# Stage a and stage b of a spectral filter, in pairs of pieces between the projections of an attention

## The chip, the cores and the metric

One core of one Trainium2 chip runs the whole kernel. The metric is the device time of one execution in microseconds; the time before is the median of three runs, 651.31 us.

## The reference

Two independent halves, both with 2048 rows and 448 columns, written side by side:

```python
# a: attention, 16 heads of 28, one shared key and value head
q = (x @ wq) -> 16 heads of 28;  k = x @ wk;  v = x @ wv
p = softmax(q k^T * 28 ** -0.5);  a = concat_heads(p v) @ wo
# b: global filter
X = rfft2(B_x)              # over rows and columns
b = irfft2(X * (w_r + 1j * w_i))
out = concatenate([a, b], axis=-1)
```

All inputs and outputs are float32.

## The kernel before

**Attention.** The queries of four heads at a time (group g, 0 to 3) are projected for 512 rows at a time (chunk c, 0 to 3). `proj` issues the matmuls (line 331): each factor is split into a rounded part and a rest, so a group with a chunk takes 11 matmuls of 128 x 512 into one PSUM bank. `evac` (lines 335 and 336) copies the bank to `qraw` on ScalarE and takes the largest magnitude of each row on VectorE into `qmx`. Keys and values ride along in spare rows of the query weights; `fetch` gathers them by DMA into `kf`, and `keys` splits the keys into `ka` (one half of the rows at a time, lines 250 to 256).

Chunk 0 is projected in the order of arrival of its inputs. For chunks 1 to 3 a loop goes over c and g, so that the count `n = 4 * (c - 1) + g` runs from 0 to 11; "group n" means this count. `split_x` prepares the next chunk's input on ScalarE (line 319) and VectorE (lines 321 and 323).

A bound on the scores is subtracted from each query. For it `qm` (line 430) is reduced from `qmx` behind group 9, `key_max` (lines 351 and 352) moves it with two small matmuls and a copy to `kmb`, `terms` (line 260) and `shift` (lines 265 and 266) form `cvec`, and `build_q` (lines 201 to 203) makes the first chunk's query: `qt`, its rounded part `qh`, its rest `ql`. `copy_q` (lines 191 to 194) puts these into the four row blocks of `qa`, on ScalarE, on VectorE and by DMA from the SP and GpSimd queues.

Behind that the main part runs over 256 steps: scores (line 780), exp on ScalarE (line 781), product with the values (line 756), with the rest of the filter and of the output placed between them by a plan written out by hand. It starts at 70.24 us.

**Filter, first part.** It is done in eight pieces q, which lie between the projections:

- `fft1_load(q)` asks for the piece `xb` (512 KB) and for its twiddle weights `fw` (128 KB) on the SP queue, lines 101 and 103.
- `fft1_fold(q)` adds and subtracts mirrored parts on VectorE in eight instructions, lines 113 to 122; it can be done in two parts, four instructions each. Its result `f` lies in one of two buffers.
- Stage a: `fft1_a_mm(q, p)` for p = 0 and 1 is a run of small matmuls (113 x 32 weights, line 138) into one PSUM bank for each p; `fft1_a_out` evacuates each with ScalarE (line 144) to `a`, which has two buffers for each p.
- Stage b: `fft1_mm(q)` multiplies `a` by `fw` (64 x 64 weights, line 157) into two banks; `fft1_out` evacuates them (line 165 on ScalarE for q below 6, line 167 on VectorE above) to `bs`, and stores `bs` to the scratch tensor `t1` from the SP queue (line 172).

Banks for projections, stage a and small matmuls come from `bank()`, which hands out six banks in turn; stage b of pieces 0 to 5 has two banks of its own (`pbb`, `po`).

**Where the pieces stand.** The order on TensorE (PE) is the order of the program text (`manual_schedule`). The other engines and the DMA queues are ordered by a planner, by readiness and text order; `behind(x, y)` tells it to issue x after y on the same engine. Behind the groups in `slots` stand stage a of one piece and stage b of the piece before:

```python
slots = (3, 5, 6, 8, 9, 10)
...
if n in slots:
    q = slots.index(n)
    fft1_a(q)
    fft1_load(q + 4)
    ...
    if q:
        fft1_b(q - 1)
    if n == 9:
        key_max()
```

Piece 6 (stage a), piece 5 (stage b), `shift` of the other chunks, piece 6 (stage b), the reduction of the bound, piece 7 (stage a) and the transposes of the values follow behind group 11 in this order on PE; stage b of piece 7 stands within the first step of the main part.

Of the kernel before, what the change touches and what calls it, by code (L numbers as in the profile page):

```python
# [55 lines left out]
def kernel(ctx: ExitStack, tc: tile.TileContext, t: dict):  # L56
# [21 lines left out]
    def behind(ins, other):  # L78

        tc.add_manual_dep(ins.ins, other.ins.name,  # L80
                          mybir.DependencyInfo(mybir.DependencyClass.NoSync, mybir.DependencyReason.DATA),
                          reason="order of issue")
# [6 lines left out]

    fc, xb, ff = {}, {}, {}
    def fft1_consts():
        fc["cs1"] = fp.tile([128, 4, 113], F32, name="cs1", tag="cs", bufs=1)
        nc.sync.dma_start(fc["cs1"], t["cs1"])

    def fft1_load(q):
        if q > 7:
            return
        x = fp.tile([128, 4, 256], F32, name="xb", tag=("wr", "b2")[q % 2])  # L100
        nc.sync.dma_start(x, t["xb"][q])
        w = fp.tile([128, 4, 64], F32, name="fw", tag=("ph", "pl")[q % 2])
        nc.sync.dma_start(w, t["fw"][:, 4 * q:4 * q + 4])
        xb[q] = x, w

    def fft1_fold(q, part=None):
        x = xb[q][0][:113]
        e2, o2 = x[:, 0:2], x[:, 2:4]
        if part != 1:
            f = ff[q] = fp.tile([113, 4, 4, 2, 32], F32, name="f", tag="wi")  # L110
            xv = x.rearrange("p k (j h m) -> p k j h m", h=2, m=32)
            for h, op in enumerate((ALU.add, ALU.subtract)):
                nc.vector.tensor_tensor(f[:, :, :, h], xv[:, :, :, 0], xv[:, :, :, 1], op=op)
            y = f.rearrange("p k j h m -> p k (j h m)")
            nc.vector.tensor_tensor(e2, y[:, 0::2], y[:, 1::2], op=ALU.add)
            nc.vector.tensor_tensor(o2, y[:, 0::2], y[:, 1::2], op=ALU.subtract)
        if part != 0:
            y = ff[q].rearrange("p k j h m -> p k (j h m)")
            return [nc.vector.tensor_tensor(y[:, 0], e2[:, 0], e2[:, 1], op=ALU.add),
                    nc.vector.tensor_tensor(y[:, 1], e2[:, 0], e2[:, 1], op=ALU.subtract),  # L120
                    nc.vector.tensor_tensor(y[:, 2], o2[:, 0], o2[:, 1], op=ALU.subtract),
                    nc.vector.tensor_tensor(y[:, 3], o2[:, 0], o2[:, 1], op=ALU.add)]

    at1, stored = {}, []

    def fft1_a(q):
        for p in range(2):
            fft1_a_out(q, p, fft1_a_mm(q, p))
# [13 lines left out]
    def fft1_a_out(q, p, pa):  # L142
        a = at1[q, p] = fp.tile([128, 2, DF], F32, name="a", tag=("pwr", "pwi")[p])
        return nc.scalar.activation(a, pa, AF.Copy)

    def fft1_b(q):
        return fft1_out(q, fft1_mm(q))

    def fft1_mm(q, pb=None):
        w = xb[q][1]  # L150
        if pb is None:
            pb = aux2("pbb"), ps_o.tile([128, 2, DF], F32, name="po")
        for p in range(2):
            a = at1.pop((q, p))
            for h in range(2):
                for e in range(2):
                    mm(pb[h][64 * e:64 * e + 64, p], w[64 * h:64 * h + 64, 2 * p + e], a[64 * h:64 * h + 64, e],  # L157
                       start=True, stop=True)
        return pb
# [36 lines left out]
    def build_q(c, g, first=False):  # L196
        cs = slice(c * CW, (c + 1) * CW)
        qh = qp.tile([128, CW], F32R, name="qh", bufs=1)
        ql = qp.tile([128, CW], F32R, name="ql", bufs=1)
        qt = ql.bitcast(F32)  # L200
        nc.vector.tensor_scalar(qt, qraw[:, g, cs], mask, cvec[:, g, c:c + 1], op0=ALU.mult, op1=ALU.add)
        nc.vector.tensor_copy(qh, qt)
        nc.vector.tensor_tensor(ql, qt, qh.bitcast(F32), op=ALU.subtract)
        if (c, g) not in qa:
            qa[c, g] = qp.tile([128, 4, CW], F32R, name="qa")
        q = qa[c, g]
        if first:
            return q, qh, ql
        for i in range(4):
            for p, src in enumerate((qh, ql)):  # L210
                mv = nc.sync.dma_start(q[32 * p:32 * p + 32, i].bitcast(F32), src[32 * i:32 * i + 32].bitcast(F32))
                behind(mv, stored[-1])
        nc.sync.dma_start(q[64:128].bitcast(F32), q[0:64].bitcast(F32))
# [15 lines left out]


    with tc.tile_pool(name="w1", bufs=1) as w1:
        kf = w1.tile([64, S], F32, name="kf")
        qm = w1.tile([128, 2], F32, name="qm")
        prod = w1.tile([128, NG, NC], F32, name="prod")
# [24 lines left out]
        def terms(c0, c1):  # L259
            return nc.vector.tensor_scalar(prod[:, :, c0:c1], qmx[:, :, c0:c1], kmb, None, op0=ALU.mult)  # L260

        def shift(c0, c1):
            b = bank()[:, :NG * (c1 - c0)]
            pb = b.rearrange("p (g c) -> p g c", g=NG)
            mm(b, blk, prod[:, :, c0:c1], start=True, stop=True)
            nc.vector.tensor_copy(cvec[:, :, c0:c1], pb)

        halves = slice(0, 1024), slice(1024, 2048)
        with tc.tile_pool(name="x1", bufs=2) as x1:
# [14 lines left out]
            def raw(src, eng):  # L284
                r = x1.tile([128, 512], F32, name="raw", bufs=8)
                eng.dma_start(r, src)
                return r
# [59 lines left out]
            def key_max():  # L347

                pb = bank()
                for k in range(2):  # L350
                    mm(pb[:, 0:1], sel[:, k], qm[:, k:k + 1], start=(k == 0), stop=(k == 1))
                nc.vector.tensor_copy(kmb, pb[:, 0:1])
# [22 lines left out]
                        proj(pq1[g], *xs[1], g, 0)  # L375
            fft1_consts()
            fft1_load(0)
            xr[2, 0] = raw(t["xa"][2, :, 0], nc.sync)
            for j in range(1, NK):
                split_x(*xs[1], 1, j)  # L380
                xr[2, j] = raw(t["xa"][2, :, j], nc.sync)
            for q in range(1, 4):
                fft1_load(q)
            fft1_fold(0)
            mask = const("mask", [128, 1], nc.sync)
            sgn = const("sgn", [128, 1], nc.sync)
# [7 lines left out]
            for c in range(1, NC):  # L394
                for g in range(NG):
                    pq = pq1[g] if c == 1 else bank()
                    for j in range(1 if c == 1 else 0, NK):
                        proj(pq, *xs[c], g, j)
                    last = evac(c, g, pq)
                    if g == 0 and c < 3:  # L400
                        parts_of(c + 1)
                        for j in range(NK):
                            split_x(*xs[c + 1], c + 1, j)
                            if c < 2:
                                xr[c + 2, j] = raw(t["xa"][c + 2, :, j], nc.sync)
                    if c == 1 and g == 1:
                        fetch(range(7), halves[0])
                    if c == 3 and g == 1:
                        fetch(range(7), halves[1])
                    if c == 2 and g == 3:  # L410
                        fetch(range(7, 14), slice(0, 1536), nc.gpsimd)
                    if c == 3 and g == 2:
                        fetch(range(7, 12), slice(1536, S), nc.gpsimd)
                    if c == 1 and g == 0:
                        fft1_fold(1)
                    if c == 2 and g == 3:
                        keys(0)
                    n = 4 * (c - 1) + g
                    if n in slots:
                        q = slots.index(n)  # L420
                        fft1_a(q)
                        fft1_load(q + 4)
                        if n == 10:

                            terms(0, 1)
                            shift(0, 1)
                            qf, qh, ql = build_q(0, 0, True)
                        if n == 9:

                            top = nc.vector.tensor_reduce(qm, qmx[:, 0:2], axis=AX.X, op=ALU.max)  # L430
                            for ins in fft1_fold(5, 1):
                                behind(ins, top)
                        if q < 6:
                            fft1_fold(q + 2, None if q not in (3, 5) else 0)
                        if q:
                            fft1_b(q - 1)
                        if n == 9:
                            key_max()
            fetch(range(12, 14), slice(1536, S), nc.gpsimd)


        behind(copy_q(0, 1, qf, ql, nc.scalar), last)
        for p in range(2):
            last = fft1_a_out(6, p, fft1_a_mm(6, p))
        for i in range(4):
            copy_q(i, 2, qf, qh, nc.sync)
            copy_q(i, 3, qf, ql, nc.gpsimd)
# [1 line left out]
        top = terms(1, NC)  # L449
        for ins in fft1_fold(7, 1):  # L450
            behind(ins, top)
        last = fft1_b(5)
        shift(1, NC)
        top = nc.vector.tensor_reduce(cmax, cvec, axis=AX.X, op=ALU.max)
        pb6 = fft1_mm(6, [pair_of(bank()) for _ in range(2)])
# [13 lines left out]
            nc.tensor.transpose(pv[:, b], kf[32:64, b * 128:(b + 1) * 128], ident[32:64, 32:64])  # L469
        fft1_out(6, pb6, bound)  # L470
        fft1_a_out(7, 1, pa7)
        nc.vector.tensor_copy(vs, pv)
        keys(1, nc.vector.tensor_copy)


    pools = ctx.enter_context(ExitStack())
# [46 lines left out]
    b2 = {}  # L523
# [494 lines left out]
```

## Time and profile before

| | us |
|---|---|
| three runs | 650.55, 651.31, 651.71 |
| profiled execution | 651.6 |
| its span, first to last instruction | 649.8 |
| TensorE busy | 642.6 (99%) |
| ScalarE busy | 555.9 (86%) |
| VectorE busy | 360.5 (55%) |
| GpSimd busy | 79.6 (12%) |
| mean granted TensorE clock | 0.998 |

Busy times are sums over the whole span; a stretch can have another limit than the mean. The changed code works between 26 and 74 us, before and at the start of the main part. PEld is TensorE's loading of weights, which overlaps its matmuls. A timeline row gives start, duration, engine, line and tiles, a count where like instructions were merged, and in brackets how long the engine had been idle and what ended that.

### The profile page before, as it was taken

The numbers are of one execution on the slowest core, as the hardware profiler recorded it, in microseconds if no ns is written. First come the engines' busy times: TensorE is split into PE (matmuls) and PEld (weight loads), VectorE is DVE, ScalarE is ACT, GpSimd is POOL, SyncE is SP. The second block draws the span as 40 slices with busy tenths as digits, with TensorE's granted clock in tenths as the row PEclk, the third lists the DMA queues.
The fourth block names the chain that finished last, engine by engine and source line by source line (L and its number), as shares of the span: only waits on it lengthen the run. The fifth ranks groups of instructions, "written<-read, shape, count | busy, mean of one in ns | idle before, by whom it ended". The sixth has DMA issues, their size and how long they took to land.

```text
span 649.8 us, 12076 instructions
## 1 busy us (share of the span) xinstructions
PE 642.6 (99%) x4470; PEld 375.8 (58%) x4470; DVE 360.5 (55%) x810; ACT 555.9 (86%) x1103; POOL 79.6 (12%) x150
## 2 busy tenths in 40 slices
PE   8999999999999999999999999999999999999996
PEld 6877554555555456554546556565656565555555
DVE  5999646778877771047765620175443510383523
ACT  5654999999999998789989988799999987899981
POOL 3022401101112100000012200011120200010010
PEclk9999999999999999999999999999999999999999
DMA  8756954534552443022062323032232313140001
GB/s 268 265 172 165 259 159 106 137 100 121 138 139 76 109 95 84 29 75 49 32 155 50 98 60 89 20 88 73 63 94 61 101 39 84 43 110 16 15 31 60
DMA packets 36114, 63.83 MB, mean 98 GB/s; under 512 B 7905, under 2 KB 23922, under 8 KB 35084
## 3 DMA queue, kind: packets, MB, share of 16 engines
q1 hardware_dynamic: 30832, 49.60, 27.6%
q0 software_dynamic: 4640, 12.48, 7.4%
q8 instruction: 36, 0.59, 0.4%
q10 hardware_dynamic: 576, 0.92, 0.4%
q14 instruction: 30, 0.25, 0.1%
HBM read 30.04 MB, written 14.75 MB: 69 GB/s over the span
## 4 chain that ended last, share of the span: by engine, by line
PE 98%; DMA 1%; ACT 0%; SPq 0%; ACTq 0%; issue 0%
PE s L780 30%; PE s L756 24%; PE po L756 7%; PE s L331 6%; PE sx L780 5%; PE po L780 4%; PE sx L756 4%; PE s L677 4%; PE s L138 2%; PE s L623 2%; PE s L611 1%; PE pbb L157 1%; DMA raw<-wq 1%; PE s L521 1%; PE s L519 1%; PE s L520 1%
## 5 line engine op out<-in xcount | busy, mean ns | idle before, releaser
L781 ACT ACTIVATE p<-s 128x512 f32<-128x512 f32 x776 | 421.9, 652 | 38.8 <-PE s L780 38.5
L780 PE MATMUL s<-qa,ka 128*128 128x512 f32 x776 | 243.8, 408 | 0.0
L780 PEld LDWEIGHTS s<-qa,ka 128*128 128x128 f32 x776 | 140.3, 188 | 80.5 <-ACT p L781 43.6
L756 PE MATMUL s<-p,vs 128*32 128x512 f32 x1408 | 163.8, 596 | 0.0
L756 PEld LDWEIGHTS s<-p,vs 128*32 128x32 f32 x1408 | 39.7, 109 | 89.5 <-issue 86.6
L781 ACT ACTIVATE p<-sx 128x512 f32<-128x512 f32 x132 | 86.1, 652 | 3.4 <-PE sx L780 3.4
L781 ACT ACTIVATE p<-po 128x512 f32<-128x512 f32 x116 | 74.9, 646 | 7.2 <-PE po L780 7.1
L658 DVE RECIPROCAL r<-r 128x128 f32<-128x128 f32 x64 | 61.0, 953 | 2.2
L684 DVE COPY ya<-s 128x448 f32<-128x448 f32 x11 | 6.9, 625 | 88.1 <-PE s L677 88.1
L780 PE MATMUL sx<-qa,ka 128*128 128x512 f32 x132 | 53.4, 405 | 0.0
L780 PE MATMUL po<-qa,ka 128*128 128x512 f32 x116 | 47.4, 408 | 0.0
L756 PE MATMUL po<-p,vs 128*32 128x512 f32 x384 | 44.9, 597 | 0.0
L631 POOL TENSOR_TENSOR yo<-y 128x226 f32<-128x226 f32 x16 | 9.6, 597 | 225.9 <-issue 214.8
L780 PEld LDWEIGHTS sx<-qa,ka 128*128 128x128 f32 x132 | 24.8, 188 | 14.0 <-ACT p L781 9.2
L647 POOL DMA_DIRECT2D ol<-ol x36 | 18.1, 508 | 105.4 <-PE s L780 55.9
L756 PE MATMUL sx<-p,vs 128*32 128x512 f32 x256 | 29.7, 596 | 0.0
L780 PEld LDWEIGHTS po<-qa,ka 128*128 128x128 f32 x116 | 21.8, 188 | 12.4 <-ACT p L781 7.0
L625 DVE COPY m<-s 128x452 f32<-128x452 f32 x15 | 9.4, 629 | 34.5 <-PE s L623 34.5
L756 PEld LDWEIGHTS po<-p,vs 128*32 128x32 f32 x384 | 10.7, 109 | 24.1 <-issue 23.4
L331 PE MATMUL s<-xh,wqh 128*128 128x512 f32 x56 | 22.7, 405 | 0.9 <-ACT wqh L311 0.9
L335 ACT ACTIVATE qraw<-s 128x512 f32<-128x512 f32 x14 | 8.1, 600 | 17.4 <-PE s L331 17.4
L331 PE MATMUL s<-xh,wql 128*128 128x512 f32 x56 | 21.6, 391 | 0.0
(211 smaller groups left out, 735.3 us busy)
## 6 DMA issues: line engine op xcount, KB each, us to landing
qa<-qa SPq DMA_DIRECT2D x15, 512.0 KB
raw<-xa SPq DMA_DIRECT2D x16, 256.0 KB
xb<-xb SPq DMA_DIRECT2D x8, 512.0 KB
qa<-qh SPq DMA_DIRECT2D x64, 64.0 KB
qa<-ql SPq DMA_DIRECT2D x60, 64.0 KB
ob<-yo SPq DMA_DIRECT2D x16, 226.0 KB
t<-bs SPq DMA_DIRECT2D x16, 225.0 KB
wr<-wr POOLq DMA_DIRECT2D x16, 225.0 KB, 4.4
```

The lines of the kernel that those rows point to most:

```text
L138: mm(pa[r0:r0 + 32, e, o0:o0 + n], f[:, 2 * r + k, 2 * p + e, h], cs1[:, 2 * r + k, :n], start=True, stop=True)
L331: mm(pq, w[:, j, gs], x[:, j], start=(j == 0 and n == 0), stop=(j == 3 and n == 1))
L335: out = nc.scalar.activation(qraw[:, g, cs], pq, AF.Copy)
L623: mm(py[:, k], z[:w, r, js], cs3[:w, k], start=True, stop=True)
L625: nc.vector.tensor_copy(m, py)
L631: nc.gpsimd.tensor_tensor(yo[:, 0:2], y1[:, 0], y1[:, 1], op=ALU.add)
L647: nc.gpsimd.dma_start(ol[c][o, g].bitcast(F32), ol[c][r, 0].bitcast(F32))
L658: nc.vector.reciprocal(r, r)
L677: mm(p, x[c][:, g, s], w, start=(g == 0 and n == 0), stop=(g == NG - 1 and n == 2))
L756: mm(po[c, g][32 * i:32 * i + 32], vs[:, kc], ps[i // 2][:, i % 2], start=(kc == 0), stop=(kc == 15))
L780: begun.append(mm(sc, ka[:, kc * 128:(kc + 1) * 128], qa[c, g][:, n], start=True, stop=True))
L781: nc.scalar.activation(ps[-1][:, n % 2], sc, AF.Exp, scale=SCALE)
```

## The change

The insertions between the projections are fewer and longer: stage a of pieces 0 and 1 behind group 5; stage a of 2 and 3, then stage b of 0 and 1, behind group 8; `key_max`, stage a of 4 and 5, then stage b of 2 and 3, behind group 10. Stage b of piece 4 goes behind group 11, between stage a of 6 and stage b of 5. The foldings and the loads of `xb` stay at the groups of `slots`.

With it come: a third buffer for folded data, used by pieces 2 and 5; folding from piece 5 on is issued behind the folding of the piece before; loads of `fw` are separate and are asked for behind the stage b that frees their buffer; stage b of pieces 1, 3 and 5 takes its two banks from the six in turn; `qh` of the first query is rounded by ScalarE instead of VectorE; `copy_q` for row blocks 1 to 3 on ScalarE is issued behind stage b of piece 5; the split of the second half of the keys is issued behind the copy of the values.

```diff
-    fc, xb, ff = {}, {}, {}
+    fc, xb, fw, ff, folded, third = {}, {}, {}, {}, {}, []
...
     def fft1_load(q):
-        if q > 7:
-            return
-        x = fp.tile([128, 4, 256], F32, name="xb", tag=("wr", "b2")[q % 2])
-        nc.sync.dma_start(x, t["xb"][q])
-        w = fp.tile([128, 4, 64], F32, name="fw", tag=("ph", "pl")[q % 2])
-        nc.sync.dma_start(w, t["fw"][:, 4 * q:4 * q + 4])
-        xb[q] = x, w
+        xb[q] = fp.tile([128, 4, 256], F32, name="xb", tag=("wr", "b2")[q % 2])
+        nc.sync.dma_start(xb[q], t["xb"][q])
+
+    def fft1_weights(q):
+        if q < 8:
+            fw[q] = fp.tile([128, 4, 64], F32, name="fw", tag=("ph", "pl")[q % 2])
+            nc.sync.dma_start(fw[q], t["fw"][:, 4 * q:4 * q + 4])
 
     def fft1_fold(q, part=None):
...
-            f = ff[q] = fp.tile([113, 4, 4, 2, 32], F32, name="f", tag="wi")
+            f = ff[q] = third[0].tile([113, 4, 4, 2, 32], F32, name="f3") if q % 3 == 2 else fp.tile(
+                [113, 4, 4, 2, 32], F32, name="f", tag="wi")
...
-                nc.vector.tensor_tensor(f[:, :, :, h], xv[:, :, :, 0], xv[:, :, :, 1], op=op)
+                ins = nc.vector.tensor_tensor(f[:, :, :, h], xv[:, :, :, 0], xv[:, :, :, 1], op=op)
+                if q > 4:
+                    behind(ins, folded[q - 1])
...
     def fft1_mm(q, pb=None):
-        w = xb[q][1]
-        if pb is None:
+        w = fw[q]
+        if pb is None and q % 2 and q < 6:
+            pb = [pair_of(bank()) for _ in range(2)]
+        elif pb is None:
             pb = aux2("pbb"), ps_o.tile([128, 2, DF], F32, name="po")
...
     def build_q(c, g, first=False):
...
-        nc.vector.tensor_copy(qh, qt)
+        if first:
+            nc.scalar.activation(qh, qt, AF.Copy)
+        else:
+            nc.vector.tensor_copy(qh, qt)
...
+                    back, forth = {5: ((), (0, 1)), 8: ((0, 1), (2, 3)), 10: ((2, 3), (4, 5))}.get(n, ((), ()))
+                    if n == 10:
+                        key_max()
+                    for q in forth:
+                        fft1_a(q)
+                    for q in back:
+                        fft1_b(q)
+                        fft1_weights(q + 4)
+                    if n == 10:
+                        terms(0, 1)
+                        shift(0, 1)
+                        qf, qh, ql = build_q(0, 0, True)
+                    if n == 9:
+                        top = nc.vector.tensor_reduce(qm, qmx[:, 0:2], axis=AX.X, op=ALU.max)
+                        for ins in fft1_fold(5, 1):
+                            behind(ins, top)
                     if n in slots:
                         q = slots.index(n)
-                        fft1_a(q)
-                        fft1_load(q + 4)
...
-                        if q:
-                            fft1_b(q - 1)
-                        if n == 9:
-                            key_max()
+                        if q < 4:
+                            fft1_load(q + 4)
+                        fft1_fold(q + 2, None if q not in (3, 5) else 0)
...
         behind(copy_q(0, 1, qf, ql, nc.scalar), last)
-        for p in range(2):
-            last = fft1_a_out(6, p, fft1_a_mm(6, p))
+        fft1_a(6)
+        fft1_b(4)
+        last = fft1_b(5)
         for i in range(4):
             copy_q(i, 2, qf, qh, nc.sync)
             copy_q(i, 3, qf, ql, nc.gpsimd)
...
-        last = fft1_b(5)
...
-        nc.vector.tensor_copy(vs, pv)
-        keys(1, nc.vector.tensor_copy)
+        last = nc.vector.tensor_copy(vs, pv)
+        behind(keys(1, nc.vector.tensor_copy), last)
```

More of the change, by code (lines that the diff above doesn't have):

```diff
@@ L97, in fft1_load @@
     def fft1_load(q):
-        if q > 7:
-            return
-        x = fp.tile([128, 4, 256], F32, name="xb", tag=("wr", "b2")[q % 2])
-        nc.sync.dma_start(x, t["xb"][q])
-        w = fp.tile([128, 4, 64], F32, name="fw", tag=("ph", "pl")[q % 2])
-        nc.sync.dma_start(w, t["fw"][:, 4 * q:4 * q + 4])
-        xb[q] = x, w
+        xb[q] = fp.tile([128, 4, 256], F32, name="xb", tag=("wr", "b2")[q % 2])
[4 more added lines that the diff above has]
+            nc.sync.dma_start(fw[q], t["fw"][:, 4 * q:4 * q + 4])
     def fft1_fold(q, part=None):
-        x = xb[q][0][:113]
+        x = xb[q][:113]
         e2, o2 = x[:, 0:2], x[:, 2:4]
         if part != 1:
-            f = ff[q] = fp.tile([113, 4, 4, 2, 32], F32, name="f", tag="wi")
+            f = ff[q] = third[0].tile([113, 4, 4, 2, 32], F32, name="f3") if q % 3 == 2 else fp.tile(
+                [113, 4, 4, 2, 32], F32, name="f", tag="wi")
             xv = x.rearrange("p k (j h m) -> p k j h m", h=2, m=32)
             for h, op in enumerate((ALU.add, ALU.subtract)):
-                nc.vector.tensor_tensor(f[:, :, :, h], xv[:, :, :, 0], xv[:, :, :, 1], op=op)
+                ins = nc.vector.tensor_tensor(f[:, :, :, h], xv[:, :, :, 0], xv[:, :, :, 1], op=op)
+                if q > 4:
+                    behind(ins, folded[q - 1])
             y = f.rearrange("p k j h m -> p k (j h m)")
@@ L118, in fft1_fold @@
             y = ff[q].rearrange("p k j h m -> p k (j h m)")
-            return [nc.vector.tensor_tensor(y[:, 0], e2[:, 0], e2[:, 1], op=ALU.add),
+            out = [nc.vector.tensor_tensor(y[:, 0], e2[:, 0], e2[:, 1], op=ALU.add),
                     nc.vector.tensor_tensor(y[:, 1], e2[:, 0], e2[:, 1], op=ALU.subtract),
@@ L122, in fft1_fold @@
                     nc.vector.tensor_tensor(y[:, 3], o2[:, 0], o2[:, 1], op=ALU.add)]
+            folded[q] = out[-1]
+            return out
     at1, stored = {}, []
@@ L231 @@
     with tc.tile_pool(name="w1", bufs=1) as w1:
+        third.append(w1)
         kf = w1.tile([64, S], F32, name="kf")
@@ L377 @@
             fft1_load(0)
+            fft1_weights(0)
             xr[2, 0] = raw(t["xa"][2, :, 0], nc.sync)
@@ L383 @@
                 fft1_load(q)
+                fft1_weights(q)
             fft1_fold(0)
@@ L418 @@
                     n = 4 * (c - 1) + g
+                    back, forth = {5: ((), (0, 1)), 8: ((0, 1), (2, 3)), 10: ((2, 3), (4, 5))}.get(n, ((), ()))
[14 more added lines that the diff above has]
+                            behind(ins, top)
                     if n in slots:
                         q = slots.index(n)
-                        fft1_a(q)
-                        fft1_load(q + 4)
[L423 to L427, printed above, removed]
-                        if n == 9:
[L430 to L434, printed above, removed]
-                        if q:
-                            fft1_b(q - 1)
-                        if n == 9:
-                            key_max()
+                        if q < 4:
+                            fft1_load(q + 4)
+                        fft1_fold(q + 2, None if q not in (3, 5) else 0)
             fetch(range(12, 14), slice(1536, S), nc.gpsimd)
         behind(copy_q(0, 1, qf, ql, nc.scalar), last)
-        for p in range(2):
-            last = fft1_a_out(6, p, fft1_a_mm(6, p))
+        fft1_a(6)
+        fft1_b(4)
+        last = fft1_b(5)
         for i in range(4):
```

## The prediction

> **What bounds the kernel now.** I read the page first, then busy time by stretch, then the chain of waits and the timelines of TensorE (PE), ScalarE (ACT), VectorE (DVE) and the SP queue around the filter's first part. The page:
>
> ```profile
> span 649.8 us, 12076 instructions
> ...
> PE 642.6 (99%) x4470; PEld 375.8 (58%) x4470; DVE 360.5 (55%) x810; ACT 555.9 (86%) x1103; POOL 79.6 (12%) x150
> ...
> PE 98%; DMA 1%; ACT 0%; SPq 0%; ACTq 0%; issue 0%
> ```
>
> PE carries 98% of the chain that ended last, so a saving must take time out of PE's stream. But 99% busy hides two things. A matmul's end is modelled, so small gaps between unlike matmuls vanish in it; and other engines are full in single stretches, as busy time by stretch shows (start and end, length, then PE, PEld, DVE, ACT, POOL, clock, DMA share, GB/s):
>
> ```profile
> 21.00:52.20 31.20, 31.20 (x404) 24.27 (x406) 31.01 (x58) 16.98 (x32) 3.50 (x7) 1.00 0.60 181
> 70.84:100.69 29.85, 29.85 (x186) 14.46 (x185) 14.87 (x27) 29.75 (x60) 4.18 (x9) 1.00 0.72 199
> ```
>
> From 21.00 to 52.20 us DVE works 31.01 of 31.20: where the changed part lies, PE and DVE are both full. From 70.84, the first exp, ACT works 29.75 of 29.85: the attention starts bound by ACT, so what counts is when the first exp starts, not when PE offers its first score. What follows is not touched: a shift of the first exp reaches the end whole.
>
> **What an insertion costs.** Two projections (L331) of PE's timeline (start, duration, what), 15 starts apart:
>
> ```profile
> 22.91 0.39 PE L331 MATMUL s<-xh,wqh 128*128 128x512 f32 x1
> ...
> 26.31 0.39 PE L331 MATMUL s<-xh,wql 128*128 128x512 f32 x1
> ```
>
> The chain in order of time (start, length), with stage a (L138) and stage b (L157) of the filter between the projections:
>
> ```profile
> 26.70 1.69 PE s L138 x64
> 28.39 5.21 PE s L331 x22
> 33.59 1.69 PE s L138 x64
> 35.28 0.34 PE pbb L157 x2
> 35.62 0.01 PE po L157 x2
> 35.63 0.18 PE pbb L157 x2
> 35.81 0.01 PE po L157 x2
> ...
> 36.20 2.72 PE s L331 x11
> ```
>
> And the weight loads of the first stage a:
>
> ```profile
> 26.63 1.51 PEld L138 LDWEIGHTS s<-cs,f 113*32 113x32 f32 x64 [0.35 <-issue]
> ```
>
> A projection starts every (26.31 - 22.91) / 15 = 0.227 us; a group of 11 takes 2.49. The 22 behind the first insertion take 5.21 where 22 steps would be 4.99: 0.22 lost to a slow restart. Stage a alone thus costs 1.69 + 0.22 = 1.91, of which its loads stream in 1.51: 0.40 is switching. The next insertion, a and b, lasts 36.20 - 33.59 = 2.61, with the same restart 2.83. Its work is 1.51 and four steps of b at 0.19, 0.76: switching is 0.56.
>
> **The change, part by part.**
> 1. Six insertions (after groups 3, 5, 6, 8, 9, 10) become three (5, 8, 10). The matmuls stay: eight a, eight b. One b (piece 4) moves from the insertions to the tail, which is no saving. Switching before: 0.40 + 5 x 0.56 = 3.20; after: 0.40 + 2 x 0.56 = 1.52. Saved: 1.68. What I can't see is the join of like with like, a behind a and b behind b. At most it costs what leaving an a does, 1.69 - 1.51 = 0.18, and what entering a b does, 0.34 - 0.19 = 0.15: three of each, 1.0. At least nothing, since one a already crosses from bank to bank within its 64 without a gap. Nearer to that, I take 0.2. PE gains 0.7 to 1.7, taken 1.5.
> 2. PE's order is by hand, so PE reaches things before DVE may have them. Rebuilt with the prices above, group 5 ends at 31.5, its insertion at 34.9, group 8 at 42.4, its insertion (two a, two b) at 47.5, group 10 at 52.5. There now stands the keys' maximum, which needs `qm` from DVE:
>
> ```profile
> 52.73 0.69 DVE L336 TENSOR_REDUCE qmx<-qraw 128x1 f32<-128x512 f32 x1 [0.53 <-ACT qraw L335]
> 53.45 0.16 DVE L430 TENSOR_REDUCE qm<-qmx 128x2 f32<-128x8 f32 x1
> ...
> 54.54 0.42 DVE L122 TENSOR_TENSOR f<-xb 113x256 f32<-113x256 f32 x1
> ...
> 62.88 0.69 DVE L203 TENSOR_TENSOR ql<-ql,qh 128x512 fp32r<-128x512 f32 x1
> ```
> ```profile
> 54.60 0.61 PE L351 MATMUL s<-qm,sel 128*128 128x1 f32 x4
> ...
> 63.44 1.75 PE L138 MATMUL s<-cs,f 113*32 113x113 f32 x64
> ...
> 70.24 1.20 PE L780 MATMUL s<-qa,ka 128*128 128x512 f32 x4
> ```
>
> DVE was full to 52.20 and then idle 0.53 for group 9's evacuation, which comes over 1 us earlier now. The same work in the same order gives `qm` at 53.61 - 0.53 = 53.1, and PE wants it at 52.5: a new stall of up to 0.6, or none if the reduction slips ahead of piece 5's folding. I take 0.3. Behind the maximum stand stage a of 4 and then of 5, at 52.8 + 0.6 + 1.5 = 54.9; piece 5 is folded at 54.96 - 0.53 = 54.4, so it holds. The third buffer is what lets piece 2 be folded before a of 0 has read its own: 0 with it; without it that folding would start at 33 or later instead of 31.
> 3. The first Q's rounding moves from DVE to ACT, where eight evacuations of the last insertion are queued ahead of it. They start when b of 2 frees a buffer, about 57.0, and take about 0.5 each (rows below), so the rounding ends near 61.7 and `ql` near 62.4 instead of 63.57. That is 1.2 earlier, about what PE gains: 0, and if the rounding is late it costs what it is late.
> 4. DMAs: the same loads and stores in number. The weights of pieces 4 and 5 are asked for behind b of 0 and 1, near 47.5, and used after 62; those of 6 behind b of 2, near 57, and used near 65. SP no longer stops at a weight load between two data loads. Third fold buffer, order of `vs` and keys at the end: nothing waits there. I take 0.
> 5. In the tail ACT decides:
>
> ```profile
> 64.83 1.05 ACT L144 ACTIVATE a<-s 128x450 f32<-128x450 f32 x2
> ...
> 66.55 0.55 ACT L165 ACTIVATE bs<-pbb 128x450 f32<-128x450 f32 x1
> ...
> 67.56 1.27 ACT L191 ACTIVATE qa<-ql 32x512 fp32r<-32x512 f32 x2
> 68.85 1.05 ACT L144 ACTIVATE a<-s 128x450 f32<-128x450 f32 x2
> 70.84 1.57 ACT L781 ACTIVATE p<-s 128x512 f32<-128x512 f32 x3 [0.94 <-PE s L780]
> ```
>
> ACT was free at 69.90 and waited 0.94 for the first score. PE would now offer that score at 70.24 - 1.5 + 0.3 = 69.0. The tail from stage a of 6 to it lasts 70.24 - 63.44 = 6.80, with b of 4 7.56, so that stage starts at 61.5. Its evacuation needs a buffer that b of 4 frees halfway: 61.5 + 1.7 + 0.7 = 63.9. From there ACT has a of 6 (1.05), b of 4 and of 5 (1.0 each, 66.55 to 67.56), three copies, all behind b of 5 now (0.64 each), and a of 7 (1.05): 6.0, to 69.9. PE's score alone would allow 69.0 + 0.6 = 69.6. So the first exp comes at 69.9, 0.9 to 1.0 earlier than 70.84; the saving beyond that is lost here. Stage a of 7 reuses a bank of b of 5, emptied at 66.5 and wanted at about 66.4: 0.1 at most.
>
> Sum: 1.5 on PE, less 0.3 at the keys' maximum, less 0.2 because ACT sets the start: 1.0. The profiled execution took 651.6, 1.8 more than its span; it becomes 650.6 with a span of 648.8. The median of the runs, 651.31, lies 0.3 under it: 650.3.
>
> [...] The trace shows 0.40 and 0.56 for each insertion, so the rows carry the sum.
>
> **The rivals.**
> A. *The whole saving arrives.* The reduction goes ahead of the folding and ACT's tail doesn't bunch. For it: ACT had 0.94 to spare. Against: the 6.0 that now stand behind piece 6. Time: 651.3 - 1.5 = 649.8, 649.6 at best.
> B. *Nothing much arrives.* DVE, full from 21.00 to 52.20, does something of low need first and PE waits for it, or the joins cost their 1.0 and the stall at the maximum its 0.6. Time: 650.8 to 651.3.
> C. *The SP queue, and slower.* The stores of pieces 4 and 5 now stand ahead of the first Q's copies in the text. Before:
>
> ```profile
> 63.97 3.33 SPq L194 DMA_DIRECT2D qa<-qh  x4
> 67.56 3.47 SPq L172 DMA_DIRECT2D t<-bs  x4
> ```
>
> If the stores are queued first, SP sits on b of 5's evacuation until 66.9, stores for 1.7 and issues the copies until 72. Before, the last was issued by 67.30 and served the fourth score at about 70.9, so landing takes 0 to 3.6. The fourth score, due at 69.7, would come at 72 to 75.6: 2.3 to 5.9 lost, 4 in the middle, 1.0 gained beside: 654.3. It decides as soon as the copies start later than before, since they then serve a score that comes 1.2 earlier. Against: their data are ready 4 us ahead of the stores', which a planner by readiness sees.
> D. *ACT's queue blocks, and slower.* Piece 2's evacuation waits at the head of ACT's queue for b of 0, which PE does only two a later, and group 9 reuses the bank that it empties. I count 0.3 to spare (0.7 to free the buffer, 0.55 to empty, against 1.6 of b on PE). With b's evacuations queued first PE waits about 1.0 behind each of two insertions: 652.3. [...]
>
> **Chances.** Forecast 0.45, A 0.22, B 0.14, C 0.09, D 0.10. The three runs lie 0.2% apart (650.55 to 651.71), so under 1.3 us can't be told from no change. The forecast, 1.0 faster, lies within that with a fifth of its cases beyond; A is beyond, B within, C and most of D slower. So faster 0.30, same 0.52, slower 0.18. The range takes in A's far end, somewhat more, and D: 649.3 to 652.4.
>
> **What would show it.** Stage a in runs of 128 matmuls at three places; group 6 starting near 34.9; a gap of 0 to 0.6 ahead of L351; the first exp at 69.9 with ACT busy before it; then the old timeline, 1.0 earlier. It is wrong if PE waits for DVE at a stage a, if group 9 or 11 waits for ACT, if a first score waits for a DMA, or if the stretch after 100 us changes its length.

## The result, and the profile after

The changed kernel takes 660.85 us (median of 5 runs, 660.26 to 663.10) against 651.33 of the kernel before, run beside it: a ratio of the means of 1.0155, 95% interval 1.0133 to 1.0176. So it is 1.3 to 1.8% slower, where 650.3 was predicted. Its profiled execution took 660.49, with a span of 658.6 against 649.8.

The page after, with the rows that answer to those shown of before (busy time and instructions; the chain that ended last):

```profile
span 658.6 us, 12072 instructions
...
PE 644.0 (98%) x4470; PEld 377.3 (57%) x4470; DVE 360.5 (55%) x809; ACT 555.1 (84%) x1104; POOL 79.2 (12%) x150
...
PE 96%; DMA 1%; SPq 1%; ACT 1%; issue 0%; ACTq 0%
```

PE has the same 4,470 matmuls and 1.4 more busy time; the other 7.4 are time in which it stood still. SPq is on the chain now with 1%, where it had 0%, a small share of a long span. The chain in order of time shows where (start, length, what carried the end):

```profile
31.32 3.23 PE s L144 x128
34.55 7.70 PE s L343 x33
42.25 3.23 PE s L144 x128
...
47.17 5.25 PE s L343 x22
52.44 0.61 ACT qraw L347
...
53.19 0.58 PE s L363 x4
53.77 3.22 PE s L144 x124
56.99 1.26 issue
...
60.47 0.56 ACT a L150
...
68.57 0.16 SPq L180
...
70.89 0.61 SPq L202
...
73.00 4.79 DMA qa<-qh
```

The first two insertions do what the change says: stage a (L144) in two runs of 128, and no stall around them. The third holds three stalls: at the keys' maximum (L363), inside stage a of piece 5, where after 124 of 128 matmuls PE waited 1.26 for nothing that the profile names ("issue"), and on ScalarE's evacuation of `a`. Then, from 68.57, the chain leaves the engines that compute: SP sends the stores of pieces 4 and 5 (L180), then the first Q's copies (L202), and the last of these lands 4.79 after SP began to issue it. ScalarE's rounding of the first Q, which the copies send; the SP queue in the same stretch; and PE from the first score (L798) on:

```profile
63.02 0.70 ACT L211 ACTIVATE qh<-ql 128x512 fp32r<-128x512 f32 x1
```
```profile
68.15 2.69 SPq L180 DMA_DIRECT2D t<-bs  x4
70.89 2.70 SPq L202 DMA_DIRECT2D qa<-qh  x4
```
```profile
74.19 0.69 PE L798 MATMUL s<-qa,ka 128*128 128x512 f32 x2 [2.72 <-DVE kl L266]
77.01 1.68 PE L798 MATMUL s<-qa,ka 128*128 128x512 f32 x2 [2.12 <-DMA qa<-qh]
...
79.05 0.58 PE L165 MATMUL pbb<-a,fw 64*64 64x225 f32 x2
```

The order on SP is turned round: before, the copies went out at 63.97 and those stores at 67.56. Now the copies' data are there at 63.72, and they go out 7.2 later, behind stores whose data come after 67. The first score waited 2.72. The trace puts that down to `kl`, which ended at the same moment, but the first experiment below shows scores that start before SP sends `kl`, which leaves the first copy. The third score waits 2.12 more, for a copy. And the matmuls of stage b, 0.36 each elsewhere, take 0.58 here. Busy time by stretch has the reason (start and end, length, PE, PEld, DVE, ACT, POOL, clock, DMA share, GB/s), after and before:

```profile
70.00:80.00 10.00, 5.01 (x52) 2.87 (x44) 3.59 (x5) 4.18 (x8) 4.68 (x9) 0.77 0.94 279
```
```profile
70.00:80.00 10.00, 10.00 (x66) 5.21 (x68) 5.32 (x8) 9.11 (x19) 3.48 (x7) 1.00 0.99 286
```

With PE idle for half of the stretch the granted clock is 0.77 instead of 1.00. That is a mean: microsecond by microsecond it is 1.00 up to about 75.5, 0.50 up to 82.3, and 1.00 again. So what follows the wait is slow as well. ScalarE's first exps show the sum:

```profile
74.76 1.09 ACT L799 ACTIVATE p<-s 128x512 f32<-128x512 f32 x2 [2.82 <-PE s L798]
...
81.16 2.06 ACT L799 ACTIVATE p<-s 128x512 f32<-128x512 f32 x4 [1.84 <-PE s L798]
```

The first is 3.9 later than before (70.84), the sixth 8.3 (81.66 against 73.33), the twelfth 8.9, and that stays to the end (8.8 in the span).

### The profile page after: what moved, and what is told of

Its sections match the earlier page's. It is cut to its first block, busy times and chain, and to the rows that moved or that the text cites. A ratio compares the mean times of both kernels' runs of the same rounds, so it can differ in the third digit from the quotient of the medians.

```text
span 658.6 us, 12072 instructions
## 1 busy us (share of the span) xinstructions
PE 644.0 (98%) x4470; PEld 377.3 (57%) x4470; DVE 360.5 (55%) x809; ACT 555.1 (84%) x1104; POOL 79.2 (12%) x150
## 4 chain that ended last, share of the span: by engine, by line
PE 96%; DMA 1%; SPq 1%; ACT 1%; issue 0%; ACTq 0%
PE s L798 30%; PE s L774 24%; PE po L774 7%; PE s L343 5%; PE sx L798 5%; PE po L798 4%; PE sx L774 4%; PE s L695 4%; PE s L641 2%; PE s L144 2%; PE s L629 1%; DMA qa<-qh 1%; PE s L539 1%; PE s L538 1%; PE s L537 1%; DMA raw<-wq 1%
## 5 line engine op out<-in xcount | busy, mean ns | idle before, releaser
L798 PE MATMUL s<-qa,ka 128*128 128x512 f32 x776 | 245.7, 410 | 5.0 <-DVE kl L266 2.7
L798 PEld LDWEIGHTS s<-qa,ka 128*128 128x128 f32 x776 | 140.9, 189 | 86.7 <-ACT p L799 43.6
L798 PE MATMUL sx<-qa,ka 128*128 128x512 f32 x132 | 53.4, 404 | 0.0
L798 PE MATMUL po<-qa,ka 128*128 128x512 f32 x116 | 47.4, 408 | 0.0
L798 PEld LDWEIGHTS sx<-qa,ka 128*128 128x128 f32 x132 | 24.8, 188 | 14.0 <-ACT p L799 9.2
L798 PEld LDWEIGHTS po<-qa,ka 128*128 128x128 f32 x116 | 21.8, 188 | 12.4 <-ACT p L799 7.0
```

The lines of the kernel that those rows point to most:

```text
L798: begun.append(mm(sc, ka[:, kc * 128:(kc + 1) * 128], qa[c, g][:, n], start=True, stop=True))
```

## The experiments

Two theories stood at the start. *The queue*: SP's order costs nearly all, and the third insertion's stalls eat what the insertions save. *The insertion*: the stalls make PE, ScalarE and the stores late, and SP's order only shows it. This table is what all runs gave; the first exp and the span are of one profiled execution and stand against 70.84 and 649.8, the ratio is that of the runs to the kernel before on the same chip.

| kernel | first exp | span | median | ratio (95%) |
|---|---|---|---|---|
| changed kernel | +3.9 | +8.8 | 660.85 | 1.0155 (1.0133 to 1.0176) |
| 1 copies first | +1.3 | +1.7 | 654.05 | 1.0049 (1.0033 to 1.0066) |
| 2 old kernel, stores first | +5.3 | +7.0 | 659.18 | 1.0123 (1.0102 to 1.0143) |
| 3 = 1, piece 7 loaded early | +0.5 | +1.6 | 653.14 | 1.0031 (1.0019 to 1.0042) |
| 4 = 1, b before a | -0.2 | +0.2 | 652.00 | 1.0018 (1.0005 to 1.0031) |
| 5 = 3, first stores late | +7.1 | +7.0 | 658.55 | 1.0118 (1.0102 to 1.0133) |
| 6 = 4, first Q early on VectorE | -1.8 | -1.0 | 650.48 | 0.9991 (0.9982 to 1.0000) |
| 7 = 6, rounding on VectorE | -1.7 | -1.6 | 650.89 | 0.9997 (0.9988 to 1.0006) |
| 8 = 6, first constants behind b | -1.9 | -0.1 | 651.06 | 0.9994 (0.9982 to 1.0007) |
| 9 = 6, both constants behind b | -1.6 | -1.6 | 650.08 | 0.9983 (0.9974 to 0.9992) |

**1. Copies first.** The loop that copies the first Q is moved ahead of `fft1_a(6)`, and the stores behind it are held behind its last copy on SP:

```
         behind(copy_q(0, 1, qf, ql, nc.scalar), last)
+        for i in range(4):
+            sent = copy_q(i, 2, qf, qh, nc.sync)
+            copy_q(i, 3, qf, ql, nc.gpsimd)
+        held.append(sent)        # later stores: behind(stored[-1], held[0])
         fft1_a(6)
```

> The changed kernel with one thing altered: on SP the four copies of the first query go ahead of the stores of pieces 4 and 5. Queue theory (the stores held the copies until 70.9, some 6 of the 9.5 us): the copies are issued near 64 to 67, the first score follows the transposes without a wait near 71.4, the first exp near 72.0, PE never idles long enough for its clock to fall; time 652 to 653.5, the rest of the loss being the three stalls of the third insertion (0.8 before the keys' maximum, 1.26 in stage a of piece 5, 0.45 before group 11). Rival (the late query itself, rounded by ACT behind eight evacuations, is what the first scores wait for): the first score stays at 73.5 or later and the time at 656 or more.

Measured: 654.05, a little above the range expected; 6.8 of the 9.5 are gone. SP's queue, and PE:

```profile
65.47 3.27 SPq L204 DMA_DIRECT2D qa<-qh  x4
68.83 4.30 SPq L180 DMA_DIRECT2D t<-bs  x6
...
74.17 1.88 SPq L270 DMA_DIRECT2D ka<-kl  x2
```
```profile
52.95 0.58 PE L365 MATMUL s<-qm,sel 128*128 128x1 f32 x4 [0.59 <-issue]
...
57.91 0.39 PE L144 MATMUL s<-cs,f 113*32 113x112 f32 x4 [1.17 <-issue]
...
60.74 0.50 PE L345 MATMUL s<-xh,wqh 128*128 128x512 f32 x1 [0.45 <-ACT a L150]
...
71.60 1.27 PE L801 MATMUL s<-qa,ka 128*128 128x512 f32 x4
```

The scores run as one block of four, at 71.60, before `kl` is sent at 74.17. The three stalls of the third insertion are still there, 0.59, 1.17 and 0.45. The queue theory holds. What is left, 0.5%, should be the third insertion's; experiments 4 and 6 test that.

**2. The old kernel, stores first.** The other half of the test: in the kernel before, the four copies on SP are issued behind the stores of piece 5, and nothing else is changed.

```
+        for i in range(4):
+            behind(copy_q(i, 2, qf, qh, nc.sync), stored[-1])   # after last = fft1_b(5)
```

> The kernel before with one thing altered: on SP the stores of piece 5 go ahead of the four copies of the first query. Queue theory: the copies are issued near 69 instead of 64, the first four scores are 4 to 6 us late, PE idles and its clock falls: 656 to 659. Rival (the queue matters only together with the new insertions): at most 652.5.

Measured: 659.18, just above the range expected and 1.2% slower, from the order on one queue. Its SP queue and PE:

```profile
60.60 7.60 SPq L172 DMA_DIRECT2D t<-bs  x6
68.30 3.12 SPq L194 DMA_DIRECT2D qa<-qh  x4
```
```profile
75.30 2.05 PE L781 MATMUL s<-qa,ka 128*128 128x512 f32 x4 [5.56 <-issue]
...
78.98 1.76 PE L781 MATMUL s<-qa,ka 128*128 128x512 f32 x4
```

```profile
70.00:80.00 10.00, 4.70 (x22) 2.79 (x23) 3.27 (x5) 2.25 (x5) 2.58 (x5) 0.67 0.91 252
```

One wait of 5.56 on PE, for which the trace names nothing ("issue"); the copies' order on SP is all that was changed. Then comes the slow clock (a mean of 0.67 from 70 to 80; 0.50 from about 73.4 to 80.2): the scores take 2.05 and 1.76 for four, where they took 1.20 before. The first exp is 5.3 later and the end 7.0, so I put about 1.7 of the price down to the clock, an estimate.

**3. Piece 7 loaded early.** The gap of "issue" inside stage a of piece 5 (1.26, and 1.17 in experiment 1) looks like PE out of program. The page of the changed kernel has 36 instruction packets on queue q8 (number, MB, share), 16 KB each; I take them for blocks of PE's program, which has 8,940 matmuls and weight loads:

```profile
q8 instruction: 36, 0.59, 0.4%
```

In the changed kernel the packet that PE lacks starts only at 55.88, when 1,146 of them had started, and PE stopped after 1,207; in the kernel before it starts at 49.34, after 940. From 50.2 to 55.6 us the DMA engines are busy 0.87 of the time. So this is experiment 1 with piece 7's 512 KB asked for behind group 7, 6 us earlier:

```
+                    if n == 7:
+                        fft1_load(7)
```

> e1_copies_first with the 512 KB of piece 7 asked for behind group 7, ahead of the stores of pieces 0 and 1 instead of behind them. Fetch theory (the gap of 1.26 in stage a of piece 5 is PE out of instructions, whose next block was queued behind the transfers that SP let go at 48 to 55): the block comes about 1 us earlier and the gap falls below 0.5, 0.8 to 1.2 us less than e1_copies_first. Rival (the gap is a wait for VectorE's folding, or for a bank): gap and time as in e1_copies_first.

Measured: 653.14. That is 0.9 under experiment 1, in the range expected, but not for the reason expected: the gap is 1.00, not under 0.5, and the packet starts at 55.19, against 55.42 in experiment 1. So the hit in time is luck. In all three kernels with the gap PE goes on 2.4 to 2.5 after the packet's start (55.88 to 58.25, 55.42 to 57.91, 55.19 to 57.59), which ties the gap to the packet. In the profiled executions the first exp came 0.8 earlier than in experiment 1 and the end only 0.1, since the filter's second part (L542) waits at 91.84 in this one; that of experiment 1 was the fastest of its runs (653.33):

```profile
57.59 0.39 PE L144 MATMUL s<-cs,f 113*32 113x112 f32 x4 [1.00 <-issue]
...
91.84 0.44 PE L542 MATMUL po<-bh,g1h 128*128 128x450 f32 x1 [0.73 <-ACT p L804]
```

**4. Stage b ahead of the keys' maximum and of stage a.** As experiment 1, with the two loops of an insertion exchanged, so that PE has 1.7 of work while VectorE finishes `qm`:

```
+                    for q in back:
+                        fft1_b(q)
+                        fft1_weights(q + 4)
                     if n == 10:
                         key_max()
                     for q in forth:
                         fft1_a(q)
```

> e1_copies_first with each insertion in the order stage b of the older two pieces, keys' maximum, stage a of the newer two. Stall theory: `qm` is there before PE asks (no wait of 0.8), the evacuations of stage a find their buffers free (no wait of 0.45 before group 11), 1.0 to 1.3 us less than e1_copies_first; the instruction gap stays, behind the same number of PE instructions (about 1217 from the start), so in the middle of stage a of piece 5 and not at its end. Rival (the gap belongs to an operand of the last matmuls of stage a): it stays at the end of stage a of piece 5.

Measured: 652.00, 2.1 under experiment 1, more than expected. The wait at the maximum, the wait on ScalarE's `a` and, not expected, the "issue" gap are all gone. In their place stands one of 1.54 at the shift of the first Q (L279, the trace names ScalarE), which is VectorE's: it copies the maximum (L366) only behind piece 6's folding.

```profile
54.23 0.60 PE L365 MATMUL s<-qm,sel 128*128 128x1 f32 x4
54.77 3.31 PE L144 MATMUL s<-cs,f 113*32 113x113 f32 x128
59.61 0.36 PE L279 MATMUL s<-prod,blk 128*128 128x4 f32 x2 [1.54 <-ACT a L150]
```
```profile
59.09 0.15 DVE L366 COPY kmb<-s 128x1 f32<-128x1 f32 x1
```

**5. The first stores late.** As experiment 3, with the stores of pieces 0 and 1 behind the fetches of keys, to empty the DMA engines from 50 to 54 us:

```
+                        kept = fetch(range(7), halves[1])
+                        for ins in stored:
+                            behind(ins, kept)
```

> The kernel of the third experiment (first Q's copies queued first, piece 7 asked for behind group 7), and in addition the four stores of pieces 0 and 1 (225 KB each), which SP issued from about 47.9 to 51.7 us, are queued behind the seven fetches of keys, which end near 57.8. So between 48 and 55 us hardly more than the small fetches is left on the DMA engines. It settles where TensorE's missing instruction block hangs: it starts to load when 1130 to 1156 TensorE instructions have started (55.2 to 55.9 us), in the kernel before and with stage b first at about 950. If data ahead of it in the DMA engines hold it up, it starts at about 950 instructions, near 50.5 us, the wait of 1.0 inside stage a of piece 5 goes, and the time falls from 653.1 by 0.5 to 1.0, to about 652.4. If it is set by how far the sequencer has got in the program, the block starts within 0.5 us of 55.2 as before, the wait stays at 1.0, and the time stays at 652.9 to 653.4.

Measured: 658.55, by a road that I had not seen. Six stores in a row hold SP from 53.58 until b of piece 2 is evacuated, and ScalarE evacuates it only from 64.38, behind the first Q's rounding. PE waits for evacuations and then for a weight load that stands behind those stores:

```profile
64.98 0.60 PE L165 MATMUL pbb<-a,fw 64*64 64x225 f32 x4 [1.07 <-ACT bs L173]
...
68.47 2.20 PE L165 MATMUL s<-a,fw 64*64 64x225 f32 x16 [2.08 <-ACT bs L173]
...
71.75 1.78 PE L165 MATMUL s<-a,fw 64*64 64x225 f32 x16 [0.55 <-DMA fw<-fw]
```

The copies go out at 70.93 again, but the first score, at 77.32, waits for none of them. So this is a price of SP's order too, on another path. For the packet it is clean all the same: PE goes through all of stage a without a gap, and the packet starts at 54.22. Of the DMA's busy shares, 50.0 to 54.0 in this kernel, and 50.2 to 55.6 and 55.6 to 57.4 in the changed one:

```profile
DMA  8979999975230000132400100522025001022201
```
```profile
DMA  8977999998866999956889999996593966937699
...
DMA  6966699096628348343432560091054200080600
...
q8 instruction: 1, 0.02, 3.2%
```

The packet starts 0.9 after PE gets past the keys' maximum (53.28) with quiet DMA engines, and 2.4 to 2.7 after it with busy ones (52.80 to 55.19, 52.95 to 55.42 and 53.19 to 55.88). Where PE does not wait there, as in experiments 4 and 6 to 9, it starts at 50.3 to 50.7. So both theories of that experiment fit in part: the start goes with the place that PE has reached in the program, and behind a wait it goes with the traffic.

**6. The first Q early on VectorE.** As experiment 4, with the copy of the maximum and the terms ahead of piece 6's second folding, and piece 7's folding behind the first Q's shift:

```
+                        top = terms(0, 1)
+                        for ins in six:            # fft1_fold(6), second part
+                            behind(ins, top)
...
+        folded[6 if first else None] = nc.vector.tensor_scalar(qt, ...)   # build_q
```

> The kernel of the fourth experiment (first Q's copies first, stage b ahead of keys' maximum and stage a), and in addition VectorE's order is changed: the copy of the keys' maximum and the terms stand ahead of the second part of piece 6's folding, and piece 7's folding stands behind the first Q's shift. In the fourth experiment TensorE waited 1.54 at the shift (59.6) since VectorE copied the maximum, ready at 54.9, only at 59.1, and ScalarE waited 3.97 for the first Q. If VectorE's order is the cause, the wait at the shift falls under 0.4, ScalarE's rounding starts before 61, the first exp comes at about 69.6 (70.68 in the fourth) and the time is 651.0 to 651.3, 0.3 faster than before. Rival: the time won is spent on the next wait, folded pieces 6 and 7 or ScalarE's own tail of 6.0 from piece 6's evacuation to the first exp; then the first exp stays at 70.3 to 70.8 and the time at 651.5 to 652.0.

Measured: 650.48, better than expected. PE has no stall left in the insertions, and the first exp comes 1.8 earlier than in the kernel before; the end of that execution only 1.0. What follows is not the old timeline: the filter's second part waits for its first load `b<-t`, which SP holds until the stores of piece 7 have landed (the waits of SP's queue, in total, times, longest). From PE, ScalarE and SP:

```profile
57.93 0.39 PE L280 MATMUL s<-prod,blk 128*128 128x4 f32 x2
...
60.85 1.75 PE L144 MATMUL s<-cs,f 113*32 113x113 f32 x64
...
89.25 0.44 PE L544 MATMUL po<-bh,g1h 128*128 128x450 f32 x1 [0.47 <-DVE bh L574]
```
```profile
63.27 0.55 ACT L150 ACTIVATE a<-s 128x450 f32<-128x450 f32 x1 [1.04 <-PE po L165]
...
69.02 3.56 ACT L806 ACTIVATE p<-s 128x512 f32<-128x512 f32 x7
```
```profile
SPq L557 <- DMA t<-bs: 7.0, 1, 7.0
```

**7. The first Q rounded on VectorE.** As experiment 6, with the change's `activation` taken back to `tensor_copy`.

> The kernel of the sixth experiment with the first Q rounded on VectorE, as the kernel before has it. It prices that part of the change. My prediction took it as neutral. If it is, the time lies within 0.3 of the sixth experiment's. If ScalarE's place is worth having, VectorE works 0.6 more between 58 and 63, piece 7's folding and the copies come that much later, and the first exp and the time are 0.3 to 0.7 later. If ScalarE is the one that sets the first exp, it has 0.6 less to do there and the time is up to 0.5 less.

Measured: 650.89 against 650.48. The medians are 0.41 apart where 0.3 had been set, but the intervals overlap, and the first exp is 0.14 later. These runs tell no difference, so the prediction's 0 stands as far as they show. In this execution `b<-t` goes out at 84.07, 0.6 ahead of experiment 6, PE does not wait for it, and the first exp, 1.7 early, reaches the end as 1.6.

**8 and 9. The second part's constants later.** As experiment 6. The constants `wr` and `wi` (225 KB a load) are loaded from about 70 to 77 us, and the last stores must land there too; from 70 to 80 us the DMA engines are busy 0.96 of the time in experiment 6. In 8 the first four of these loads, in 9 the first eight are issued by SP behind the second part's loads:

```
-                ld = nc.gpsimd.dma_start(b2[n, q][...], t[n][...])
-                behind(ld, begun[-1])
+                ld = (nc.sync if q < 1 else nc.gpsimd).dma_start(b2[n, q][...], t[n][...])   # 9: q < 2
+                behind(ld, loaded if q < 1 else begun[-1])
```

> The kernel of the sixth experiment, and the first pair of constants of the filter's second part (wr and wi, four loads of 225 KB) is asked for by SP behind the second part's first loads b<-t, not by POOL at 70 to 72 us. In the sixth experiment the first exp came 1.82 earlier than before (69.02), but the end only 1.2: SP waited 7.0 for the stores of piece 7 to land while those constants filled the DMA engines, the loads went out at 84.66 and TensorE waited at the second part's first matmuls (89.25). If that is the next bound, b<-t goes out before 82, the wait at those matmuls goes, the offset of 1.8 reaches the end, and the time is 649.6 to 650.2. Rival: the offset is lost elsewhere between 90 and 105 us, for example on the constants themselves, which land later and are wanted near 91; then the time stays at 650.3 to 650.9, or goes above it.

> As the eighth experiment, with the second pair of constants (four more loads of 225 KB) on SP behind the second loads of b as well. It takes all 1.8 MB from the stretch of 70 to 77 us. If the DMA engines' load is what delays the stores, b<-t goes out another 1 to 3 us earlier than in the eighth, with nothing more to gain in time: within 0.3 of the eighth. If the second pair lands late for VectorE's products near 95, it is 0.3 to 1.5 slower than the eighth.

Measured: 8 misses its range. It gives 651.06 (649.44 to 653.47), not apart from experiment 6; `b<-t` goes out at 80.95 instead of 84.66 and the wait at 89 is gone, but VectorE then waits 2.80 for the second load, and PE 1.46 at 103. 9 gives 650.08, 1.0 under 8 where at most 0.3 was expected: a miss as well. It is 0.17% under the kernel before with an interval that excludes 1. Its loads go out at 77.54, and the offset of the first exp, 1.6, is that of the end. SP in 8 and in 9, and VectorE in 8:

```profile
80.95 1.76 SPq L557 DMA_DIRECT2D b<-t  x4
```
```profile
77.54 1.76 SPq L557 DMA_DIRECT2D b<-t  x4
```
```profile
98.00 0.40 DVE L575 CAST bh<-b 128x450 fp32r<-128x450 f32 x1 [2.80 <-DMA b<-t]
```

So with SP's order, PE's and VectorE's order around the insertion and the constants' loads set right, the changed kernel is 1.1 us under the kernel before. How much of that is the constants' is not shown, since the intervals of experiments 6 to 9 overlap; what they alone would do in the kernel before was not tried.

## Why the prediction was wrong

**The step that failed is part 4, "I take 0" for the DMAs.** Rival C named the mechanism and the place, and got a chance of 0.09. The argument against it was that the copies' data are ready 4 us ahead of the stores' and that a planner by readiness sees that. They were ready, at 63.72, and SP sent nothing from 65.70 to 68.15, yet its queue kept the order of the text. Experiments 1 and 2 price it from both kernels: 6.8 (660.85 to 654.05) and 7.8 (659.18 against 651.41).

**Rival C's size was short too**, 2.3 to 5.9 with 4 in the middle. The copies were issued until 73.6 where I had "until 72", and the last landed 4.2 after that where I had at most 3.6, so the fourth score came at 77.93, past C's 72 to 75.6. The rest is the clock, which I had nowhere. Microsecond by microsecond it is 1.00 or 0.50 in these traces, and it is 0.50 for about 6.8 us in or behind PE's waits: from 75.5 in the changed kernel, from 73.4 in experiment 2, from 68.7 in experiment 5. The means over 70 to 80 us (0.77, 0.67, 0.72) differ only in how much of that they take in. Before the fall stood one wait of 5.56 in experiment 2, but in the changed kernel one of 2.72 with the start of the next, 0.7 behind it, and in experiment 5 one of 1.07 with one of 2.08, which ended at 68.47. The waits of 0.59, 1.17 and 0.45 in experiment 1, from 52 to 61 us, left it at 1.00: the mean of that execution is 0.998, as in the kernel before, where it is 0.50 only in the last 3.2 us. So shorter waits close together came before a fall as well; from what length on, these runs do not show.

**Part 2, the stall at the keys' maximum**, was right in its cause and the order of the queues, and sized short: 0.79 against "up to 0.6" and 0.3 taken. `qm` came at 52.93 to 53.09, as the 53.1 that I had worked out; PE was 0.1 earlier than 52.5. Missed is the gap of 1.26 behind it, more than the wait itself: that PE can stand still in the midst of a run, for what I take to be a block of its program, was in no term and no rival. The 36 packets for 8,940 matmuls and weight loads make about 248 to a packet, an estimate that takes all of them for PE's.

**Rival D** came in small: ScalarE's queue, with evacuations of a and b taking turns, cost PE 0.45 once, at the third insertion, where I had priced 1.0 at each of two. That ScalarE's queue can hold back what is ready shows in experiment 5: it stood idle for 2.30 up to the first Q's rounding at 62.34, while b of piece 2, through on PE at 58.1, was evacuated only from 64.38.

**Part 1 was right.** The first pair of stages a carries 3.23 of the chain where two alone carried 1.69 each, so the joins cost nothing. From the first insertion to group 6 are 3.23, and to group 9 from the second 4.92, against 3.4 and 5.1 worked out. In experiment 6, where nothing stalls, stage a of piece 6 starts at 60.85; I had 61.5 with 0.3 for the stall, and that execution was 0.2 ahead from the start (the projections' 22.87 against 23.08).

**Part 3** was neutral as far as experiment 7 tells. Its times were off: ScalarE's evacuations began at 59.60, not 57.0, and the rounding ended at 63.72, not 61.7, behind PE's stalls; in experiment 1 no score waited for it. **Part 5** was right in its working, but on a path that no longer mattered: in experiment 6 ScalarE needs 5.75 from piece 6's evacuation to the first exp (63.27 to 69.02; I had 6.0), and had no wait before it.

**"A shift of the first exp reaches the end whole"** fell as well. Of 3.9 late 8.8 arrived, by the later copies and the clock. Of 1.8 early in the profiled execution of experiment 6 only 1.0 arrived, since PE waited at the second part's first load; in that of experiment 7, with this load 0.6 earlier, 1.6 of 1.7 did. So the second part's loads are close to the next bound, and the medians (0.6 and 0.2 under the kernel before) are too near each other to price it.

What stays open: which event starts the packet ahead of PE's gap. Its start follows the wait at the maximum in four kernels, but no run moved that wait by a known amount alone.

## What to carry to other kernels

When an edit moves a producer's code past a consumer's, write out the new order of every DMA queue, SP's first. Here SP's queue kept its order and held copies whose data were there at 63.72 until 70.89, behind stores whose data came after 67, and the tensor engine paid waits of 2.72 and 2.12 and, from 75.5, 6.8 us at a clock of 0.50. So a long wait on a full engine was not only its own length: a first exp 3.9 late became an end 8.8 late. And an earlier start can meet the next transfer that the old one hid, as in experiment 6, where 1.8 early became 1.0; look for it before the gain is counted.

## What the hardware showed that was not expected

- PE stood still in the midst of a run of matmuls, after 124 of 128 (after 1,207 matmuls and weight loads in the changed kernel), for 1.00 to 1.26 us in three kernels, and went on 2.4 to 2.5 after a 16 KB packet, taken for a block of its instructions, had started. That packet started 0.9 after a wait of PE's with quiet DMA engines and 2.4 to 2.7 after it with busy ones.
- A copy of 64 KB took 4.79 us from the start of its issue to landing, with the DMA engines busy 0.94 of the time from 70 to 80 us. That is not new with the change: the profile has 3.6 to 4.8 for the copies into `qa` in the kernel before.
- The granted clock was 1.00 or 0.50, and 0.50 for about 6.8 us around PE's waits (from 75.5, 73.4 and 68.7); the longest single wait before it fell was 2.72 in the changed kernel, 5.56 in experiment 2 and 2.08 in experiment 5. Four scores at 0.50 took 1.76 to 2.07 instead of 1.20.
